# RWKV-5 attention and SwiGLU on one Trainium2 core: unpadded k and r tiles, and another order of the first steps

## The chip, the cores and the metric

The kernel runs on one core of one Trainium2 chip. The metric is the device time of one execution in microseconds (us). The kernel before took 755.13 us, the median of three runs (754.04 to 755.39).

## The reference

The first half is a linear attention with a decay for each channel, over 4 batches, 8 heads, 768 positions and head dimension 48. The second half is a SwiGLU block over the 3072 rows of 384 that come out of it, with a hidden width of 1536.

```
state = zeros(B, H, D, D)
for t in range(S):                      # B, H, S, D = 4, 8, 768, 48
    cur = einsum('bhd,bhe->bhde', u * k[t], v[t])
    y[t] = einsum('bhd,bhde->bhe', r[t], state + cur)
    state = w * state + einsum('bhd,bhe->bhde', k[t], v[t])
x = y.transpose(0, 2, 1, 3).reshape(B * S, H * D)        # 3072 x 384
g = x @ w_gate                                           # 384 x 1536
out = (g * sigmoid(g) * (x @ w_val)) @ w_out             # 1536 x 384
```

The three weight matrices come as 64-bit floats, and the kernel makes 32-bit floats of them by work on their bits ("rounding").

## The kernel before, in words

The 768 positions are cut into 6 chunks of 128; with 4 batches that makes N = 24 tiles, tile i being chunk i // 4 of batch i % 4. For each tile the kernel does this, with all 8 heads side by side, two heads to a pair:

- `load` (L95) and `load_v` (L101) issue the DMAs of k, r and v on SP's queue. k and r come in rows of 48 numbers, 8 heads to a position; in the tile each head has 64 columns, 48 of data and 16 of zeros, so a pair fills 128 partitions once turned.
- `prepare` (L223), on POOL (GpSimd): khat = k * kscale and rhat = r * rscale (powers of the decay and their inverses, tables made at the start), rk = r * k and rk * u; then DVE (VectorE) sums rk to du, one number for each head and position.
- `turn` (L244): PE (TensorE) transposes khat and rhat, ACT (ScalarE) copies them to kT and rT. kT holds each head of a pair in its own half of the partitions, with zeros in the other.
- `diagonal` (L237): POOL fills At with du on its diagonal (identity times du, 128 x 1024).
- `scores` (L259), in two halves: PE multiplies kT and rT, DVE writes the results over At where the mask allows.
- `outputs` (L272): PE makes the tile's output from At and v, and from rT and the state Z; ACT copies it to xT.
- `update` (L299): PE makes khat times v, DVE adds it to Z, POOL scales Z by wL.

Two tiles make a group g of 256 rows for the second half. `gate_value` (L324) is one piece: 128 columns of the hidden width, 6 matmuls with wg and wv into one of two PSUM buffers (gv), a sigmoid on ACT, two products on DVE (L339, L340) into hT. `project` (L344) is a third of the output of one tile. A group has 12 gate/value pieces and 6 projection parts.

The weights are loaded in 18 chunks of 768 KB with three buffers (w_bits). `round_weights` (L137) takes one chunk through two instructions on ACT (w_mag, w_low: L151, L152), two on DVE (L155, L156) and an add on POOL (L157), all issued in one call, and then loads another chunk. The chunks come in the order of use: gate and value in turns for 256 columns, then the output matrix.

The order is written by hand, in the last loop of `fast`, over steps s (L375). Each engine runs its instructions in the order of the program. Step s does the diagonal of tile s - 1, prepares tile s + 1, turns tile s, scores tile s - 1, makes the outputs and the update of tile s - 2; in odd steps from 3 on it queues a new group. Between these parts there are five gaps, in which `feed` takes pieces from the front of one list, at most 3 a step in steps 3 to 7, 5 in steps 8 and 9, then 12. Two gaps round one chunk each, and `gate_value` rounds ahead of itself what it needs.

Of the kernel before, what the change touches and what calls it, by code (L numbers as in the profile page):

```python
# [15 lines left out]
P = 128  # L16
# [6 lines left out]
def fast(  # L23
# [26 lines left out]
    DP = 64  # L50
# [16 lines left out]
    wcol = cst.tile([P, HP], FP32, name="wcol")  # L67
    ub = cst.tile([P, H, D], FP32, name="ub")
    kscale = cst.tile([P, H, DP], FP32, name="kscale")
    rscale = cst.tile([P, H, DP], FP32, name="rscale")  # L70
    wL = cst.tile([P, HP, 2 * D], FP32, name="wL")
    sq = cst.tile([P, 8, HP], FP32, name="sq")
    bad = cst.tile([P, HP], FP32, name="bad")
    held = cst.tile([P, HP], FP32, name="held")
    badc = cst.tile([P, 1], FP32, name="badc")
    ones = cst.tile([P, 1], FP32, name="ones")
# [7 lines left out]
    Z = [cst.tile([P, HP, 2 * D], FP32, name=f"Z{b}") for b in range(B)]  # L84
    r_ld = [cst.tile([P, H, DP], FP32, name=f"r_ld{i}") for i in range(2)]
    k_ld = [cst.tile([P, H, DP], FP32, name=f"k_ld{i}") for i in range(2)]

    v_ld = [cst.tile([P, HP, VW], FP32, name=f"v_ld{i}") for i in range(4)]
    khat = [cst.tile([P, H, DP], FP32, name=f"khat{i}") for i in range(4)]
    rhat = [cst.tile([P, H, DP], FP32, name=f"rhat{i}") for i in range(2)]  # L90
    At = [cst.tile([P, H, P], FP32, name=f"At{i}") for i in range(2)]

    kT = [cst.tile([P, HP, 2, P], FP32, name=f"kT{i}") for i in range(2)]

    def load(i):  # L95
        c, b = divmod(i, B)
        rows = slice(P * c, P * (c + 1))
        for src, dst in ((k, k_ld[i % 2]), (r, r_ld[i % 2])):
            sp.dma_start(out=dst[:, :, 0:D], in_=src[b, :, rows, :].rearrange("h t d -> t h d"))
# [22 lines left out]
    AHEAD = 3  # L122
    bits = {}
    state = {"loaded": 0, "rounded": 0}

    def load_weights():
        n = state["loaded"]
        if n == len(chunks):
            return
        state["loaded"] += 1  # L130
        src = chunks[n][0].bitcast(INT32)
        bits[n] = three.tile([P, WN, 2], INT32, name="w_bits", tag="w_bits")
        sp.dma_start(
            out=bits[n][:].rearrange("p (c f) two -> p c (f two)", c=src.shape[1]), in_=src
        )

    def round_weights(count):  # L137

        for _ in range(count):
            n = state["rounded"]
            if n == len(chunks):
                return
            state["rounded"] += 1
            x = bits.pop(n)
            lo, hi = x[:, :, 0], x[:, :, 1]
            dst = chunks[n][1].bitcast(INT32)
            mag = two.tile([P, WN], INT32, name="w_mag", tag="w_mag")
            low = two.tile([P, WN], INT32, name="w_low", tag="w_low")  # L150
            act.activation(mag[:].bitcast(FP32), hi.bitcast(FP32), AF.Abs, scale=float(2.0**-112))  # L151
            act.activation(low[:], lo.bitcast(UINT32), AF.Copy, scale=float(2.0**-29))  # L152
            c = dst.shape[1]
            mag, low, hi = (t.rearrange("p (c f) -> p c f", c=c) for t in (mag[:], low[:], hi))
            dve.tensor_scalar(dst, hi, -(1 << 31), None, ALU.bitwise_and)  # L155
            dve.scalar_tensor_tensor(dst, mag, 3, dst, ALU.logical_shift_left, ALU.bitwise_or)  # L156
            pool.tensor_tensor(dst, dst, low, ALU.add)  # L157
            load_weights()


    pool.memset(wcol[:], 1.0)
    for t in k_ld + r_ld:
        dve.memset(t[:, :, D:DP], 0.0)
    for t in v_ld:
        dve.memset(t[:, :, D:64], 0.0)
    for e in range(2):
        sp.dma_start(out=wcol[64 * e : 64 * e + D, :], in_=w.rearrange("(a e) d -> e d a", e=2)[e])
# [6 lines left out]
    for n in range(AHEAD):  # L174
        load_weights()

    make_identity(nc, ident[:])
    dve.tensor_scalar(held[:], wcol[:], W_LOW, W_HIGH, ALU.max, ALU.min)
# [3 lines left out]
    pw = two.tile([P, HP, P + 1], FP32, name="pw", tag="hT")  # L182
    ipw = two.tile([P, HP, P], FP32, name="ipw", tag="hT")
    dve.memset(pw[:, :, P : P + 1], 1.0)
    dve.tensor_copy(pw[:, :, P - 1 : P], held[:].unsqueeze(2))
    for l in range(7):
        n = 1 << l
        f = sq[:, l, :].unsqueeze(2).to_broadcast([P, HP, n])
        dve.tensor_mul(pw[:, :, P - 2 * n : P - n], pw[:, :, P - n : P], f)
    dve.reciprocal(ipw[:], pw[:, :, 0:P])  # L190
    for src, dst in ((pw[:, :, 1 : P + 1], kscale), (ipw[:], rscale)):
        t_ps = ps_a.tile([P, HP, P], FP32, name="t_ps", tag="a")
        for a in range(HP):
            pe.transpose(t_ps[:, a, :], src[:, a, :], ident[:])
        act.copy(dst[:].rearrange("p h d -> p (h d)"), t_ps[:].rearrange("p a x -> p (a x)"))  # L195
    pool.memset(wL[:], 0.0)
    for e in range(2):
        q = slice(64 * e, 64 * e + 64)
        dve.tensor_copy(
            wL[q, :, D * e : D * (e + 1)], sq[q, 7, :].unsqueeze(2).to_broadcast([64, HP, D])  # L200
        )
# [6 lines left out]
    for t in kT:  # L208
        for e in range(2):
            pool.memset(t[64 * e : 64 * e + 64, :, 1 - e, :], 0.0)  # L210
# [10 lines left out]
    dus, turned = {}, {}  # L221

    def prepare(i):  # L223
        kl, rl = k_ld[i % 2], r_ld[i % 2]
        rk = two.tile([P, H, D], FP32, name="rk", tag="rk")
        pool.tensor_mul(khat[i % 4][:], kl[:], kscale[:])  # L226
        pool.tensor_mul(rhat[i % 2][:], rl[:], rscale[:])  # L227
        pool.tensor_mul(rk[:], rl[:, :, 0:D], kl[:, :, 0:D])  # L228
        pool.tensor_mul(rk[:], rk[:], ub[:])  # L229
        du = three.tile([P, H], FP32, name="du", tag="du")  # L230
        dve.tensor_reduce(du[:], rk[:], axis=AX.X, op=ALU.add)  # L231
        dus[i] = du
        load_v(i)
        if i + 2 < N:
            load(i + 2)

    def diagonal(i):  # L237

        pool.tensor_mul(  # L239
            At[i % 2][:], ident[:].unsqueeze(1).to_broadcast([P, H, P]),  # L240
            dus.pop(i)[:].unsqueeze(2).to_broadcast([P, H, P]),
        )

    def turn(i):  # L244
        for nm, t in (("kT", khat[i % 4]), ("rT", rhat[i % 2])):
            tp = ps_a.tile([P, HP, P], FP32, name="tp", tag="a")
            for a in range(HP):
                pe.transpose(  # L248
                    tp[:, a, :], t[:, 2 * a : 2 * a + 2, :].rearrange("p e d -> p (e d)"), ident[:]
                )  # L250
            if nm == "kT":
                for e in range(2):
                    q = slice(64 * e, 64 * e + 64)
                    act.copy(kT[i % 2][q, :, e, :], tp[q])  # L254
            else:
                turned[i] = three.tile([P, HP, P], FP32, name=nm, tag=nm)
                act.copy(turned[i][:], tp[:])
# [41 lines left out]
    def update(i):  # L299
# [4 lines left out]
        ps = ps_a.tile([P, HP, 2 * D], FP32, name="u_ps", tag="a")  # L304
        for a in range(HP):
            pe.matmul(  # L306
                ps[:, a, :].rearrange("p (e d) -> p e d", e=2),
                kh[:, 2 * a : 2 * a + 2, :].rearrange("p e d -> p (e d)"),
                bass.AP(
                    tensor=vl.tensor, offset=vl[:, a, 0:1].offset,  # L310
                    ap=[list(vl[:].ap[0]), [64, 2], [1, D]],
                ),
                start=True, stop=True, skip_group_check=True,
            )
        if c == 0:
            dve.tensor_mul(z[:], ps[:], wL[:])
        else:
            dve.tensor_add(z[:], ps[:], z[:])  # L318
            pool.tensor_mul(z[:], z[:], wL[:])  # L319


    hT = {}

    def gate_value(g, f):  # L324
        if g == 0:
            round_weights(2 * (f // 2) + 4 - state["rounded"])
# [17 lines left out]
    def project(g, j, part):  # L344
        c, b = divmod(2 * g + j, B)
        round_weights(len(chunks) - state["rounded"])
# [15 lines left out]
    todo = deque()  # L362

    def feed(n):
        for _ in range(min(n, len(todo))):
            todo.popleft()()

    def queue(g):
        for f in range(FC):
            todo.append(lambda g=g, f=f: gate_value(g, f))  # L370
            if g > 0 and f >= 2 and f < 8:
                todo.append(lambda g=g, n=f - 2: project(g - 1, n // 3, n % 3))

    prepare(0)
    for s in range(N + 2):  # L375

        per = [0] * 5 if s < 3 else [1, 0, 1, 0, 1] if s < 8 else [1] * 5 if s < 10 else [3, 2, 2, 3, 2]
        if 1 <= s <= N:
            diagonal(s - 1)
        if s + 1 < N:  # L380
            prepare(s + 1)
        if s < N:
            turn(s)
        round_weights(1 if s else 0)
        feed(per[0])
        if 1 <= s <= N:
            scores(s - 1, 0)
            feed(per[1])
            scores(s - 1, 1)
            feed(per[2])  # L390
        if s >= 2:
# [3 lines left out]
            feed(per[3])  # L395
            update(s - 2)
        round_weights(1 if s > 1 else 0)
        feed(per[4])
    feed(len(todo))
    for j in range(2):  # L400
        for part in range(3):
            project(N // 2 - 1, j, part)
# [413 lines left out]
```

## Time and profile before

| what | value |
|---|---|
| median of the runs | 755.13 us |
| the profiled execution | 753.81 us |
| its span, from the first to the last instruction | 752.1 us |
| PE busy in the span | 704.4 us |
| POOL, DVE, ACT busy | 203.6, 218.1, 153.9 us |
| mean granted TensorE clock | 0.981 |

Times in rows of the trace are microseconds from the span's start, or ns where "mean" is said. A row of groups reads: line, engine, operation, output from inputs, shapes, count, then busy time and mean ns of one, then the idle time of that engine just before them and what ended it. A row of waits reads: who waited for whom, us in total, times, longest. PEld is the loading of the stationary operand, which overlaps PE. One fp32 matmul leaves two records, so a gate/value piece of six matmuls shows as x12. An engine that is idle off the path to the end costs nothing.

### The profile page before, as it was taken

Reading aid. Unit: us, or ns where it says so; the run is one execution under the profiler, and the core shown is the slowest. Engines: PE = TensorE matmul, PEld = TensorE weight load, DVE = VectorE, ACT = ScalarE, POOL = GpSimd, SP = SyncE. Lnnn points to the kernel's source line nnn. Section 1 sums busy time; section 2 is a strip of 40 time slices with the busy share of each in tenths; the row PEclk is TensorE's granted clock in tenths of the full one; section 3 lists DMA queues with packets and bytes.
Section 4 is the critical chain, followed back from the end, with each engine's and each line's share of the span. In section 5 each row is a group of like instructions: output and inputs, shape, how many; then the busy total and the mean of one; then the engine's idle time right before and its main releaser. Section 6 shows DMA issues by size and latency. Waiting matters only on the chain.

```text
span 752.1 us, 10222 instructions
## 1 busy us (share of the span) xinstructions
PE 704.4 (94%) x4298; PEld 563.0 (75%) x4298; DVE 218.1 (29%) x448; ACT 153.9 (20%) x305; POOL 203.6 (27%) x168
## 2 busy tenths in 40 slices
PE   2775978999999999999999999999999999999997
PEld 1654867878878778778778778778778778777773
DVE  4255654523222222223123213123213212212120
ACT  2541634311112111102111112111112112111110
POOL 5865667650303030303030303030302311000000
PEclk9988989999999999999999999999999999999999
DMA  8565555121102020102020201020100000000000
GB/s 213 112 152 147 165 161 156 32 43 33 32 11 43 1 43 11 31 11 43 1 53 1 44 11 31 12 42 5 38 22 1 23 12 2 12 10 2 10 11 24
DMA packets 85767, 33.98 MB, mean 45 GB/s; under 512 B 76368, under 2 KB 79568, under 8 KB 85712
## 3 DMA queue, kind: packets, MB, share of 16 engines
q1 hardware_dynamic: 82256, 28.52, 16.2%
q10 hardware_dynamic: 3456, 4.72, 1.8%
q8 instruction: 36, 0.59, 0.3%
q14 instruction: 19, 0.16, 0.1%
HBM read 28.51 MB, written 4.72 MB: 44 GB/s over the span
## 4 chain that ended last, share of the span: by engine, by line
PE 85%; POOL 6%; DVE 5%; issue 2%; ACT 1%; DMA 0%; SPq 0%; DVEq 0%; POOLq 0%
PE gv L332 48%; PE o_ps L351 25%; PE y_ps L293 4%; PE s_ps L263 4%; PE tp L248 2%; PE u_ps L306 2%; POOL At L239 2%; POOL rhat L227 1%; POOL khat L226 1%; POOL rk L229 1%; POOL rk L228 1%; DVE wv L156 1%; DVE wg L156 1%; DVE wv L155 1%; DVE wg L155 1%
## 5 line engine op out<-in xcount | busy, mean ns | idle before, releaser
L332 PE MATMUL gv<-xT,wg 128*128 128x256 f32 x864 | 217.5, 389 | 19.1 <-DVE hT L340 16.8
L332 PE MATMUL gv<-xT,wv 128*128 128x256 f32 x864 | 212.7, 383 | 0.0
L332 PEld LDWEIGHTS gv<-xT,wg 128*128 128x128 f32 x864 | 161.5, 193 | 50.4 <-issue 20.0
L351 PE MATMUL o_ps<-wo,hT 128*128 128x384 f32 x576 | 197.4, 487 | 0.6 <-ACT o_sb L357 0.6
L332 PEld LDWEIGHTS gv<-xT,wv 128*128 128x128 f32 x864 | 166.7, 193 | 23.5
L339 DVE TENSOR_TENSOR sg<-sg,gv 128x256 f32<-128x256 f32 x144 | 60.5, 420 | 359.3 <-ACT sg L338 359.3
L351 PEld LDWEIGHTS o_ps<-wo,hT 128*128 128x128 f32 x576 | 107.7, 190 | 62.0 <-ACT o_sb L357 1.2
L338 ACT ACTIVATE sg<-gv 128x256 f32<-128x256 f32 x144 | 55.3, 384 | 427.2 <-PE gv L332 427.2
L319 POOL TENSOR_TENSOR Z<-Z,wL 128x384 f32<-128x384 f32 x16 | 16.5, 1032 | 342.2 <-DVE Z L318 342.2
L340 DVE TENSOR_TENSOR hT<-sg,gv 128x256 f32<-128x256 f32 x144 | 60.5, 420 | 4.9
L239 POOL TENSOR_TENSOR At<-ident,du 128x1024 f32<-128x1024 f32 x24 | 45.5, 1898 | 37.6 <-PE y_ps L293 37.6
L263 PEld LDWEIGHTS s_ps<-rT,kT 128*128 128x128 f32 x384 | 50.4, 197 | 7.0 <-DVE At L267 0.7
L263 PE MATMUL s_ps<-rT,kT 128*128 128x128 f32 x384 | 51.0, 281 | 0.3 <-DVE At L267 0.3
L267 DVE COPY_PREDICATED At<-mask,s_ps 128x512 f32<-128x512 int32 x48 | 34.0, 732 | 41.5 <-PE s_ps L263 41.5
L231 DVE TENSOR_REDUCE du<-rk 128x8 f32<-128x384 f32 x24 | 13.3, 553 | 100.0 <-POOL rk L229 100.0
L293 PE MATMUL y_ps<-At,v_ld 128*32 128x128 f32 x768 | 36.7, 283 | 5.2 <-issue 2.8
L293 PEld LDWEIGHTS y_ps<-At,v_ld 128*32 128x32 f32 x768 | 30.4, 113 | 6.5 <-issue 3.6
L226 POOL TENSOR_TENSOR khat<-k_ld,kscale 128x512 f32<-128x512 f32 x24 | 30.5, 1271 | 5.4 <-ACT kscale L195 5.4
L227 POOL TENSOR_TENSOR rhat<-r_ld,rscale 128x512 f32<-128x512 f32 x24 | 30.6, 1274 | 2.0 <-ACT outside L218 2.0
L254 ACT COPY kT<-tp 64x512 f32<-64x512 f32 x48 | 27.9, 580 | 12.6 <-PE tp L248 11.3
L293 PE MATMUL y_ps<-rT,Z 128*32 128x128 f32 x480 | 30.1, 279 | 0.0
L293 PEld LDWEIGHTS y_ps<-rT,Z 128*32 128x32 f32 x480 | 19.3, 109 | 8.3 <-issue 7.8
(60 smaller groups left out, 318.4 us busy)
## 6 DMA issues: line engine op xcount, KB each, us to landing
k_ld<-in_k_dram SPq DMA_DIRECT2D x24, 192.0 KB, 3.1
r_ld<-in_r_dram SPq DMA_DIRECT2D x24, 192.0 KB, 3.5
w_bits<-in_moe_w_gate_dram SPq DMA_DIRECT2D x6, 768.0 KB, 4.6
w_bits<-in_moe_w_val_dram SPq DMA_DIRECT2D x6, 768.0 KB, 4.6
v_ld<-in_v_dram SPq DMA_DIRECT2D x48, 96.0 KB, 2.7
w_bits<-in_moe_w_out_dram SPq DMA_DIRECT2D x6, 768.0 KB, 4.3
out_dram<-o_sb ACTq DMA_DIRECT2D x24, 192.0 KB, 1.9
ub<-in_u_dram SPq DMA_DIRECT2D x1, 192.0 KB, 4.5
```

Of the source, the lines that this page charges most:

```text
L226: pool.tensor_mul(khat[i % 4][:], kl[:], kscale[:])
L227: pool.tensor_mul(rhat[i % 2][:], rl[:], rscale[:])
L239: pool.tensor_mul(At[i % 2][:], ident[:].unsqueeze(1).to_broadcast([P, H, P]), dus.pop(i)[:].unsqueeze(2).to_broadcast([P, H, P]),)
L254: act.copy(kT[i % 2][q, :, e, :], tp[q])
L263: pe.matmul(ps[:, n, :], kT[i % 2][:, a, e, :], turned[i][:, a, :], start=True, stop=True, skip_group_check=True,)
L267: dve.copy_predicated(At[i % 2][:, 4 * half : 4 * half + 4], mask[:].bitcast(INT32).unsqueeze(1).to_broadcast([P, HP, P]), ps[:],)
L293: pe.matmul(ps[32 * q : 32 * q + 32, cc, :], *rows[q][n], start=(n == 0), stop=(n == len(rows[q]) - 1), skip_group_check=True,)
L332: pe.matmul(gv[:, o, :].rearrange("p (i t) -> p i t", i=2), wt[:, c, P * f : P * (f + 1)], xT[:, 2 * g % NX : 2 * g % NX + 2, c, :], start ...
L338: act.activation(sg[:], gv[:, 0, :], AF.Sigmoid)
L339: dve.tensor_mul(sg[:], sg[:], gv[:, 0, :])
L340: dve.tensor_mul(hT[g][:, f, :], sg[:], gv[:, 1, :])
L351: pe.matmul(ps[:], hT[g][:, f, P * j : P * (j + 1)], wo[:, f, :], start=(f == 0), stop=(f == FC - 1),)
```

## The change

Everything is in `fast`; the general path behind it is not touched.

**Unpadded tiles.** k, r, khat, rhat, kscale and rscale have 48 columns for each head, so a turned pair fills 96 partitions; wcol, wL, Z, kT and rT have 96 partitions. The products on POOL run over 384 columns, not 512. [...] Memsets of the padding and of kT go.

**Tables.** Both tables are turned from the same powers pw, and the reciprocal is taken by DVE behind the transpose, from PSUM, over 384 columns. Before, DVE took it ahead of the transpose over 512.

**u products.** `prepare` is split: `own_product` (rk, rk * u, du) and `scale` (khat, rhat, loads). For tiles 0 and 1 the u products stand ahead of the first khat; afterwards ahead of khat of the same tile.

**Diagonal.** For tiles 0 to 5 the diagonal is made by eight activations on ACT, one a head, from then on by POOL as before.

**Rounding.** It is cut into three parts with a counter each; one call does POOL's part of a chunk that has its DVE part, DVE's part of the next one, and ACT's part of one further on. The load of another chunk is issued with DVE's part.

**Order of pieces.** The list is searched for the first piece whose weights have been issued (`need`), so pieces of group 1 run between those of group 0. Groups 0 and 1 have no projection parts between their pieces; those of group 0 follow all at once, ahead of group 2. A table says for each gap of steps 0 to 8 whether to round (R) or to feed (F): five pieces a step from step 4.

```diff
-    DP = 64
+    D2 = 2 * D
...
+    def round_act():
+        n = next_chunk("act")
+        if n is not None:
...
+            act.activation(
+                mags[n][:].bitcast(FP32), hi.bitcast(FP32), AF.Abs, scale=float(2.0**-112)
+            )
+            act.activation(lows[n][:], lo.bitcast(UINT32), AF.Copy, scale=float(2.0**-29))
...
+    def round_weights():
+
+        if done["dve"] > done["pool"]:
+            round_pool()
+        if done["act"] > done["dve"]:
+            round_dve()
+        round_act()
...
+    own_product(0)
+    own_product(1)
...
     def diagonal(i):
 
-        pool.tensor_mul(
-            At[i % 2][:], ident[:].unsqueeze(1).to_broadcast([P, H, P]),
-            dus.pop(i)[:].unsqueeze(2).to_broadcast([P, H, P]),
-        )
+        du = dus.pop(i)
+        if i < 6:
+            for h in range(H):
+                act.activation(At[i % 2][:, h, :], ident[:], AF.Identity, scale=du[:, h : h + 1])
+        else:
...
                 for e in range(2):
-                    q = slice(64 * e, 64 * e + 64)
-                    act.copy(kT[i % 2][q, :, e, :], tp[q])
+                    act.activation(
+                        kT[i % 2][:, :, e, :], tp[0:D2], AF.Identity, scale=own[:, e : e + 1]
+                    )
...
     def feed(n):
-        for _ in range(min(n, len(todo))):
-            todo.popleft()()
+        for _ in range(n):
+            ready = [k for k, (need, _) in enumerate(todo) if need <= done["pool"]]
+            if ready:
+                todo.pop(ready[0])[1]()
...
+    EARLY = [
+        ("R", "", "", "", "R"),
...
+        ("R", "", "RF", "F", "F"),
+        ("RF", "F", "RF", "F", "F"),
...
-        per = [0] * 5 if s < 3 else [1, 0, 1, 0, 1] if s < 8 else [1] * 5 if s < 10 else [3, 2, 2, 3, 2]
```

What stands on PE from the outputs of tile 1 (step 3) to the outputs of tile 2 (step 4), before: tp are the transposes, s_ps the scores, y_ps the outputs, u_ps the update, and a pair of gv rows (wg, wv) is one piece.

```order
L293 MATMUL y_ps<-At_114,v_ld_104 32x128 x16
L306 MATMUL u_ps<-v_ld_104,khat_108 128x96 x4
L332 MATMUL gv<-xT,wg 128x256 x3
L332 MATMUL gv<-xT,wv 128x256 x3
L248 MATMUL tp<-ident,khat_107 128x128 x4
L248 MATMUL tp<-ident,rhat_111 128x128 x4
L332 MATMUL gv<-xT,wg 128x256 x3
L332 MATMUL gv<-xT,wv 128x256 x3
L263 MATMUL s_ps<-rT,kT_116 128x128 x8
L332 MATMUL gv<-xT,wg 128x256 x3
L332 MATMUL gv<-xT,wv 128x256 x3
L293 MATMUL y_ps<-At_113,v_ld_105 32x128 x16
```

And in the changed kernel, from the step's transposes on:

```order
L285 MATMUL tp<-ident,khat_108 96x128 x4
L285 MATMUL tp<-ident,rhat_112 96x128 x4
L366 MATMUL gv<-xT,wg 128x256 x3
L366 MATMUL gv<-xT,wv 128x256 x3
L299 MATMUL s_ps<-rT,kT_117 128x128 x4
L366 MATMUL gv<-xT,wg 128x256 x3
L366 MATMUL gv<-xT,wv 128x256 x3
L299 MATMUL s_ps<-rT,kT_117 128x128 x4
L366 MATMUL gv<-xT,wg 128x256 x3
L366 MATMUL gv<-xT,wv 128x256 x3
L329 MATMUL y_ps<-At_114,v_ld_106 32x128 x16
```

Between the transposes and the outputs of step 4 there are three pieces where there were two, one of them between the score halves, and two follow behind the outputs.

What stands on ACT in step 3, before (w_mag and w_low are a chunk's rounding, sg the sigmoid):

```order
L254 COPY kT_116<-tp 64x4x128 x2
L257 COPY rT<-tp 128x512
L151 ACTIVATE w_mag<-w_bits 128x768
L152 ACTIVATE w_low<-w_bits 128x768
L297 COPY xT<-y_ps 128x384
L151 ACTIVATE w_mag<-w_bits 128x768
L152 ACTIVATE w_low<-w_bits 128x768
L338 ACT_TABLE_LOAD
L338 ACTIVATE sg<-gv 128x256
```

And now:

```order
L271 ACTIVATE At_114<-ident,du 128x128 x8
L288 ACTIVATE kT_117<-tp,own 96x4x128 x2
L293 COPY rT<-tp 96x512
L151 ACTIVATE w_mag<-w_bits 128x768
L154 ACTIVATE w_low<-w_bits 128x768
L151 ACTIVATE w_mag<-w_bits 128x768
L154 ACTIVATE w_low<-w_bits 128x768
L333 COPY xT<-y_ps 128x384
L372 ACT_TABLE_LOAD
L372 ACTIVATE sg<-gv 128x256 x2
```

Eight instructions of the diagonal have come ahead, both chunks stand ahead of the copy to xT, and two sigmoids follow it instead of one.

What stands on POOL behind the start, before (rk_... rows are the u products):

```order
L226 TENSOR_TENSOR khat_107<-k_ld_101,kscale 128x512
L227 TENSOR_TENSOR rhat_111<-r_ld_99,rscale 128x512
L228 TENSOR_TENSOR rk<-r_ld_99,k_ld_101 128x384
L229 TENSOR_TENSOR rk<-rk,ub 128x384
L226 TENSOR_TENSOR khat_108<-k_ld_102,kscale 128x512
L227 TENSOR_TENSOR rhat_112<-r_ld_100,rscale 128x512
L228 TENSOR_TENSOR rk<-r_ld_100,k_ld_102 128x384
L229 TENSOR_TENSOR rk<-rk,ub 128x384
L239 TENSOR_TENSOR At_113<-ident,du 128x1024
```

And now:

```order
L187 TENSOR_TENSOR rk<-r_ld_100,k_ld_102 128x384
L188 TENSOR_TENSOR rk<-rk,ub 128x384
L187 TENSOR_TENSOR rk<-r_ld_101,k_ld_103 128x384
L188 TENSOR_TENSOR rk<-rk,ub 128x384
L260 TENSOR_TENSOR khat_108<-k_ld_102,kscale 128x384
L261 TENSOR_TENSOR rhat_112<-r_ld_100,rscale 128x384
L260 TENSOR_TENSOR khat_109<-k_ld_103,kscale 128x384
L261 TENSOR_TENSOR rhat_113<-r_ld_101,rscale 128x384
L172 TENSOR_TENSOR wg<-wg,w_low 128x3x256
```

The u products of tiles 0 and 1 have come ahead of the first khat, and where the diagonal stood there is now the add of the first chunk.

More of the change, by code (lines that the diff above doesn't have):

```diff
@@ L121, in fast @@
     WN = 6 * P
-    AHEAD = 3
-    bits = {}
-    state = {"loaded": 0, "rounded": 0}
-    def load_weights():
[L127 to L134, printed above, removed]
-        )
[L137 to L147, printed above, removed]
+    NW = len(chunks)
@@ L148, in round_weights, with round_dve @@
+    def round_dve():
+        n = next_chunk("dve")
+        if n is not None:
             dst = chunks[n][1].bitcast(INT32)
[L149 to L152, printed above, removed]
             c = dst.shape[1]
-            mag, low, hi = (t.rearrange("p (c f) -> p c f", c=c) for t in (mag[:], low[:], hi))
+            hi = bits.pop(n)[:, :, 1].rearrange("p (c f) -> p c f", c=c)
+            mag = mags.pop(n)[:].rearrange("p (c f) -> p c f", c=c)
@@ L218, in fast, with scale @@
     act.copy(outside, n_ps[0:1, 0, 0:1])
[L221 to L232, printed above, removed]
+    turned = {}
+    def scale(i):
+        pool.tensor_mul(khat[i % 4][:], k_ld[i % 2][:], kscale[:])
+        pool.tensor_mul(rhat[i % 2][:], r_ld[i % 2][:], rscale[:])
         load_v(i)
@@ L394, in fast @@
                 queue((s - 3) // 2)
[L395 removed]
+            gap(s, 3)
             update(s - 2)
[L397 to L398 removed]
+        gap(s, 4)
+    assert done["pool"] == NW
     feed(len(todo))
[L400 to L402 removed]
+    for p in range(6):
+        project(N // 2 - 1, p // 3, p % 3)
 @with_exitstack
```

174 lines of the change are left out of this document (112 added, 62 removed).

## The prediction

> **What bounds the kernel now.** I read the stretches first, cut where TensorE stops waiting (at 123.6 us); columns: busy us of PE, PEld, DVE, ACT, POOL with instruction counts, then granted clock, DMA share and GB/s.
>
> ```profile
> 0.00:123.60 123.60, 83.77 (x618) 69.98 (x619) 58.89 (x109) 50.21 (x77) 82.06 (x72) 0.90 0.60 155
> 123.60:752.10 628.50, 620.67 (x3680) 493.02 (x3680) 159.16 (x340) 103.68 (x228) 121.50 (x97) 1.00 0.10 24
> 20.00:40.00 20.00, 13.85 (x104) 11.82 (x103) 6.04 (x9) 9.34 (x14) 15.21 (x12) 0.91 0.57 118
> ```
>
> Behind 123.6 us PE is busy 620.67 of 628.50 us at clock 1.00: only less work there, or work done sooner, shortens that part. Ahead of it PE is idle for 40 us and runs at clock 0.90, and no engine is full (POOL 82 of 124). So a loop of waits sets the pace. The chain, one step of it:
>
> ```profile
> 46.07 1.90 POOL At L239
> 47.97 1.22 POOL khat L226
> 49.19 1.22 POOL rhat L227
> 50.41 0.97 POOL rk L228
> 51.45 1.00 POOL rk L229
> 52.48 0.55 DVE du L231
> 53.03 0.87 DVE wv L155
> 54.00 0.96 DVE wv L156
> 54.95 1.29 DVE At L267 x2
> 56.24 0.44 DVE Z L316
> 58.78 1.72 issue
> 60.50 1.90 POOL At L239
> ```
>
> POOL does the diagonal and the four products, DVE waits for the last of them (du), then does both rounding chunks of the step in its queue, and POOL's adds of these chunks (under "issue") come before the next diagonal. The step takes 60.50 - 46.07 = 14.4 us and each lap crosses POOL, DVE and POOL again. The waits of the same stretch say it too (us in total, times, longest):
>
> ```profile
> DVE du L231 <- POOL rk L229: 58.3, 9, 8.3
> ```
>
> Then the chain where PE takes over, whose pieces are also my prices of PE work (a gate/value piece is x12, two tiles of transposes x8, both score halves x16, one update x8), and one output tile without the state term from the timeline:
>
> ```profile
> 105.18 4.89 PE gv L332 x12
> 110.07 0.87 PE tp L248 x8
> 110.95 2.59 PE gv L332 x12
> 113.54 1.78 PE s_ps L263 x16
> 117.92 1.73 PE y_ps L293 x55
> 123.62 4.21 PE gv L332 x12
> 142.73 0.86 PE u_ps L306 x8
> 62.29 1.10 PE L293 MATMUL y_ps<-At,v_ld 128*32 128x128 f32 x32
> ```
>
> A piece costs 2.59 us, but 4.89 or 4.21 right after a wait. From the order, by 123.62 us PE has done steps 0 to 6, and of step 7 its transposes, scores, outputs and update (scores 0 to 6, outputs 0 to 5, updates 0 to 5), and 12 pieces.
>
> **The change part by part.** *The loop.* Staging puts a chunk's three parts in three successive calls, so POOL's adds are of a chunk that DVE finished earlier. In steps 1 to 6 the diagonal (1.90) leaves POOL for ACT; khat and rhat fall from 512 to 384 columns, the width of rk, so from 1.22 to about 0.96.
>
> ```profile
> L157 POOL TENSOR_TENSOR wv<-wv,w_low 128x768 int32<-128x768 int32 x6 | 10.9, 1822 | 13.7 <-DVE wv L156 13.7
> L151 ACT ACTIVATE w_mag<-w_bits 128x768 f32<-128x768 f32 x18 | 16.5, 916 | 13.6 <-DVE wv L156 6.5 <-DVE wg L156 5.2 <-DVE wo L156 1.8
> L152 ACT ACTIVATE w_low<-w_bits 128x768 int32<-128x768 uint32 x18 | 16.4, 911 | 6.1 <-POOL wv L157 2.6 <-POOL wg L157 2.5 <-POOL wo L157 1.0
> L254 ACT COPY kT<-tp 64x512 f32<-64x512 f32 x48 | 27.9, 580 | 12.6 <-PE tp L248 11.3
> L297 ACT COPY xT<-y_ps 128x384 f32<-128x384 f32 x24 | 11.5, 479 | 57.8 <-PE y_ps L293 57.8
> L338 ACT ACTIVATE sg<-gv 128x256 f32<-128x256 f32 x144 | 55.3, 384 | 427.2 <-PE gv L332 427.2
> L340 DVE TENSOR_TENSOR hT<-sg,gv 128x256 f32<-128x256 f32 x144 | 60.5, 420 | 4.9
> ```
>
> POOL's step with two chunks: 0.96 x 2 + 0.97 + 1.00 + 1.82 x 2 = 7.5 us. ACT's: two chunks 2 x (0.92 + 0.91) = 3.65, kT and rT three times 0.58 = 1.75 (I take 1.9, because two of them now carry a scale by partition), and eight new 128x128 instructions for the diagonal. No row shows one. 384 columns take 0.479 and 256 take 0.384, so 128 would be 0.28 by that slope (8 x 0.28 = 2.2 us); the upper end is the 256-column price, 8 x 0.384 = 3.1. I take 2.7, the middle, because the slope knows no per-partition scale. ACT's step is 3.65 + 1.9 + 2.7 = 8.25 us and ACT, not POOL, becomes the fullest engine of steps 1 to 3. The Trainium skill ("ScalarE: Activation LUTs", section "What ACT_TABLE_LOAD costs") charges 186 ns plus 0.833 ns a column, 93 ns more for each pointer operand, and lets neighbours overlap by 93 ns; that is about 2.3 us for the eight, and the sum would come out about 1.2 us lower. No run here shows such an instruction yet.
>
> *The start.* The first rounding on ACT now stands behind the cast of the flag, and the flag's matmul behind DVE's reciprocal and two du, which wait for POOL's four early products. All of ACT is queued behind this cast.
>
> ```profile
> 7.94 1.09 PE L194 MATMUL t_ps<-ident,pw 128*128 128x128 f32 x4 [7.94 <-DVE pw L189]
> L190 DVE RECIPROCAL ipw<-pw 128x512 f32<-128x512 f32 x1 | 3.4, 3354 | 0.0
> 11.57 0.16 DVE L213 TENSOR_TENSOR bad<-held,wcol 128x4 f32<-128x4 f32 x1
> 12.88 0.14 ACT L218 CAST outside<-n_ps 1x1 int32<-1x1 f32 x1
> ```
>
> Both table transposes now follow each other, to about 7.94 + 2 x 1.09 = 10.1; the reciprocal of 384 columns is 3.35 x 384/512 = 2.5, to 12.6; wL at Z's price 0.5, two du 1.1, to 14.2; from "bad" to the end of the cast it took 13.02 - 11.57 = 1.45 with a wait in it, I take 1.0: ACT is free at 15.2 us.
>
> *The first piece.* From there ACT does chunk 0 (1.8), kT and rT (1.9), chunks 1 and 2 (3.65), to 22.5; three steps of 8.25, to 47.3; two copies of outputs (0.96), to 48.2. The second of these copies ends the wait of the first gate/value piece. What ACT still waits for comes on top: in the rows above it waited 13.6 + 6.1 = 19.7 us on 18 chunks, 1.1 each, or 9.9 us on the nine chunks here. Staging removes most of that; I keep 1.8. So the first piece starts at 50 us, bounds 46.7 (no waits, diagonal at 2.2) and 58 (all waits). Before, it started at 44.8:
>
> ```profile
> 44.82 1.49 PE L332 MATMUL gv<-xT,wg 128*128 128x256 f32 x6
> ```
>
> The early steps thus gain nothing by themselves; three times two chunks are rounded earlier in exchange.
>
> *Steps 4 to 8.* Five pieces a step from two groups, instead of three: PE 5 x 2.59 + 0.87 + 1.78 + 1.73 + 0.86 = 18.2 us a step. ACT with three chunks: 5.5 + 1.9 + 2.7 + 0.48 + 5 x 0.384 = 12.5; POOL 9.4; both below 18.2, so PE sets the pace and the waits of the loop hide under it. The tightest place is the step's first sigmoid: ahead of it on ACT stand the diagonal 2.7, kT and rT 1.9 and a chunk 1.83, then come the sigmoid 0.38 and DVE's two products 0.84, 7.7 us in all from the step's start; the third piece wants the same buffer at 0.87 + 2 x (2.59 + 0.89) = 7.8. That is no margin, so I take 2 us of waits over these steps.
>
> *Catching up.* At 50 us PE has done four transposes, three scores, two outputs and one update. It has left, to the state of 123.62 us: 12 x 2.59 + 4 transposes 3.5 + 4 scores 7.1 + outputs 2 x 1.10 + 2 x 1.73 = 5.7 + 5 updates 4.3 = 51.6 us. The first piece follows a wait and pays 4.89 - 2.59 = 2.3 once; in exchange the piece at 123.62 (4.21) runs at 2.59, 1.6 less.
>
> *The rest.* Unpadding leaves PE's moving columns as they are (128 in transposes and scores, 96 in updates), so PE's work stays. DMA runs stay 48 numbers at the source: I cost it at nothing. On SP's queue the loads of chunks 3 and 4 now stand ahead of v of tile 2 and k, r of tile 4, not behind; v of tile 2 is read two steps later, k of tile 4 by POOL in step 3, some 15 us on, so the queue hides it. The kT copies grow from 64 to 96 partitions, same columns; ACT is busy 103.68 of 628.50 there and hides it. Pieces done early empty the list sooner: a new group then starts right behind its outputs, which cost this:
>
> ```profile
> PE gv L332 <- ACT xT L297: 2.4, 4, 0.6
> ```
>
> The list (39 items done at the end of step 9, not 23; 24 offered and 18 added in two steps) first runs dry in step 15, not 19: two more waits of 0.6, 1.2 us.
>
> *Sum.* 50.0 + 51.6 + 2.3 + 2.0 + (628.5 - 1.6) + 1.2 = 734.0 us of span against 752.1, so 18.1 less. The profiled run took 753.8 with its 1.7 around the span: 735.7. The median shown, 755.1, lies 1.3 higher: 737.
>
> **The rivals.** *Late and ragged:* ACT keeps its old waits, the first piece starts at 58, and the sigmoids in steps 4 to 8 cost PE up to 4 us more than I took: 745 to 749. For it: w_low needs the buffer that POOL's add two chunks earlier frees, so ACT still waits on POOL. Against: POOL has only 7.5 us of work in a step of 8.25.
>
> *Light ACT:* diagonal at its lower bound, no waits: first piece at 46.7, no raggedness, 737 - 3.3 - 2.0 = 731.7, some us less if the piece starts warm.
>
> *DMA sets the pace (slower):* what 123.6 us of loads brought, 155 GB/s x 123.6 us = 19.2 MB, must now come by about 106 us, 181 GB/s; and by 50 us the first nine chunks, six k, six r, four v and u:
>
> ```profile
> w_bits<-in_moe_w_gate_dram SPq DMA_DIRECT2D x6, 768.0 KB, 4.6
> k_ld<-in_k_dram SPq DMA_DIRECT2D x24, 192.0 KB, 3.1
> ```
>
> (9 x 768 + 17 x 192 KB, about 10.4 MB, 215 GB/s.) If the queue can't bring more than the 155 GB/s of before, the gain is gone: 19.2 MB end at 124 us again, 755; at 145 GB/s they end at 132 us, 763. That is the point from which it decides. Against: DMA was busy only 0.60 of the time at 155, which makes 258 GB/s at full share; the worst stretch, 118 GB/s at 0.57, still makes 207, and 10.4 MB at 207 GB/s take 50 us, just where ACT ends anyway.
>
> **How the numbers follow.** A difference of 0.2% (1.5 us) is about what a measurement of this kernel tells from no change. Chances: forecast (731 to 742) 0.62, light ACT below that 0.08, late and ragged 0.20, DMA at its old rate within 0.2% 0.04, slower 0.06. So faster 0.90, same 0.04, slower 0.06. The range 729 to 749 covers the bounds of the first piece and the ragged case, and leaves out the DMA cases and a lucky start.
>
> **What would show it.** Right: first gv near 50 us; POOL's At absent before the seventh; PE 0.95 busy or more from then on at clock 1.00; step pitch about 8 us in steps 1 to 3 and 18 in steps 4 to 7; PE still busy for some 620 us behind its state of 123.62; six waits for xT. Wrong: gv waiting for hT by several us a step; ACT waiting for DMA of w_bits; or eight diagonals well over 3.1 us.

## The result and the profile after

| what | before | after |
|---|---|---|
| median of 4 runs each | 755.26 us | 736.34 us |
| lowest and highest | 754.04 to 755.65 | 735.78 to 738.54 |
| the profiled execution, its span | 753.81, 752.1 us | 738.54, 736.8 us |
| mean granted TensorE clock | 0.981 | 0.981 |

The ratio of the times is 0.9758 (95% interval 0.9735 to 0.978): 18.9 us faster. The forecast was 737.0, in a range of 729 to 749. The profiled execution of after is the highest of its four, 2.2 us above the median; all rows of after below are of this execution.

The stretches of after, cut at 20 and 40 us, then at the first gate/value piece (47.60) and at the piece (123.92) that stands nearest to the cut of before at 123.6. Columns as in the prediction.

```profile
20.00:40.00 20.00, 13.08 (x94) 11.94 (x93) 14.21 (x16) 18.13 (x40) 19.76 (x14) 0.66 0.99 256
47.60:123.92 76.32, 70.64 (x476) 61.75 (x477) 43.25 (x69) 37.57 (x77) 38.16 (x28) 0.95 0.44 116
123.92:736.80 612.88, 603.93 (x3660) 477.20 (x3660) 146.13 (x320) 96.34 (x216) 106.31 (x93) 1.00 0.09 22
```

Where before needed 628.5 us from 123.6 to its end, after needs 612.88 from 123.92, 15.6 less. By then it has done 19 gate/value pieces where before had 12, but not yet the outputs and the update of step 7: 7 x 2.59 - 1.73 - 0.86 = 15.5 us of PE's work done sooner. Ahead of 123.92 PE is idle for 31.7 us where before it was for 40, and 26 of them lie ahead of the first piece; from there to 123.92 PE is busy 70.64 of 76.32 us, or 0.93. But look at POOL between 20 and 40 us: 19.76 of 20, where before it had 15.21. ACT, which the forecast took for the fullest engine, has 18.13.

One lap of the early steps on the chain of work that ended last (start, duration, engine, what):

```profile
28.35 1.67 POOL rk L187
...
30.10 1.01 POOL rk L188
31.10 0.95 POOL khat L260
32.05 0.95 POOL rhat L261
33.01 0.87 POOL wv L172
...
33.97 1.49 issue
35.46 1.82 POOL wg L172
37.29 1.68 POOL rk L187
```

The lap is 37.29 - 28.35 = 8.94 us, and every row of it is POOL's or POOL's "issue". The chain no longer crosses to DVE and ACT. The waits of PE, in total, times, longest:

```profile
PE gv L366 <- ACT xT L333: 9.9, 8, 5.8
PE gv L366 <- DVE hT L374: 5.1, 2, 4.2
```

The long wait for xT ends at the first piece, the long wait for hT at 123.92. Behind 130 us the trace has six waits for xT, 0.6 us each.

Two pieces follow a long wait and are slow, and the update has become shorter (chain rows):

```profile
47.60 5.49 PE gv L366 x12
71.03 0.68 PE u_ps L342 x8
123.92 5.27 PE gv L366 x12
```

### The profile page after: what moved, and what is told of

The parts are those of the page before. It is cut to its first block, busy times and chain, and to the rows that moved or that the text cites. A ratio compares the mean times of both kernels' runs of the same rounds, so it can differ in the third digit from the quotient of the medians.

```text
span 736.8 us, 10255 instructions
## 1 busy us (share of the span) xinstructions
PE 696.1 (94%) x4298; PEld 558.2 (76%) x4298; DVE 223.4 (30%) x443; ACT 165.1 (22%) x352; POOL 184.0 (25%) x159
## 4 chain that ended last, share of the span: by engine, by line
PE 88%; POOL 5%; issue 2%; DMA 1%; DVE 1%; ACT 1%; SPq 0%; POOLq 0%
PE gv L366 49%; PE o_ps L384 25%; PE y_ps L329 5%; PE s_ps L299 5%; PE tp L285 2%; PE u_ps L342 2%; DMA r_ld<-in_r_dram 1%; POOL rk L187 1%; POOL wo L172 1%; POOL wg L172 1%; POOL rhat L261 1%; POOL rk L188 1%; POOL khat L260 1%; ACT xT L333 1%; DVE wo L164 0%
## 5 line engine op out<-in xcount | busy, mean ns | idle before, releaser
L355 POOL TENSOR_TENSOR Z<-Z,wL 96x384 f32<-96x384 f32 x16 | 16.1, 1008 | 359.4 <-DVE Z L354 359.4
L299 PEld LDWEIGHTS s_ps<-rT,kT 96*128 96x128 f32 x384 | 52.5, 204 | 6.3 <-ACT rT L293 0.3
L299 PE MATMUL s_ps<-rT,kT 96*128 96x128 f32 x384 | 52.8, 287 | 0.0
L273 POOL TENSOR_TENSOR At<-ident,du 128x1024 f32<-128x1024 f32 x18 | 34.1, 1894 | 38.0 <-PE y_ps L329 38.0
L288 ACT ACTIVATE kT<-tp,own 96x512 f32<-96x512 f32 x48 | 30.1, 675 | 1.3 <-PE tp L285 0.5
L329 PE MATMUL y_ps<-rT,Z 96*32 96x128 f32 x480 | 30.2, 278 | 0.0
L187 POOL TENSOR_TENSOR rk<-r_ld,k_ld 128x384 f32<-128x384 f32 x24 | 27.6, 1148 | 4.3 <-DMA r_ld<-in_r_dram 4.3
L390 ACT COPY o_sb<-o_ps 128x384 f32<-128x384 f32 x24 | 11.5, 479 | 73.7 <-PE o_ps L384 73.7
L260 POOL TENSOR_TENSOR khat<-k_ld,kscale 128x384 f32<-128x384 f32 x24 | 24.0, 999 | 13.3 <-PE u_ps L342 13.3
L333 ACT COPY xT<-y_ps 128x384 f32<-128x384 f32 x24 | 11.5, 478 | 63.7 <-PE y_ps L329 63.7
```

Of the source, the lines that this page charges most:

```text
L187: pool.tensor_mul(rk[:], rl[:], kl[:])
L260: pool.tensor_mul(khat[i % 4][:], k_ld[i % 2][:], kscale[:])
L273: pool.tensor_mul(At[i % 2][:], ident[:].unsqueeze(1).to_broadcast([P, H, P]), du[:].unsqueeze(2).to_broadcast([P, H, P]),)
L288: act.activation(kT[i % 2][:, :, e, :], tp[0:D2], AF.Identity, scale=own[:, e : e + 1])
L299: pe.matmul(ps[:, n, :], kT[i % 2][:, a, e, :], turned[i][:, a, :], start=True, stop=True, skip_group_check=True,)
L329: pe.matmul(ps[32 * q : 32 * q + 32, cc, :], *rows[q][n], start=(n == 0), stop=(n == len(rows[q]) - 1), skip_group_check=True,)
```

## The experiments

Each is an edit of the kernel after, unless it says otherwise. The times are medians, the ratios are to the kernel before, run beside them on the same chip.

| run | time us | ratio, 95% interval |
|---|---|---|
| after | 736.34 | 0.9758 [0.9735, 0.978] |
| e1_narrow_only | 745.17 | 0.9884 [0.9864, 0.9904] |
| e2_three_pieces | 734.71 | 0.9737 [0.9721, 0.9753] |
| e3_unstaged | 734.41 | 0.9733 [0.9717, 0.9749] |
| e4_diagonal_on_pool | 741.59 | 0.9828 [0.9812, 0.9845] |
| e5_act_diagonal_to_8 | 735.70 | 0.9746 [0.973, 0.9763] |
| e6_without_kr_loads | 736.34, one execution | |
| e8_unstaged_diagonal_to_8 | 731.14 | 0.9688 [0.9672, 0.9704] |
| e9_narrow_and_act_diagonal | 735.24 | 0.974 [0.9724, 0.9757] |
| e10_old_order_diagonal_to_8 | 732.85 | 0.9704 [0.9687, 0.972] |
| e11_four_w_low | 730.72 | 0.9681 [0.9664, 0.9697] |
| e12_unstaged_to_8_three_w_low | 731.01 | 0.9684 [0.9668, 0.9701] |

### Narrow tiles alone (e1)

The kernel before with the unpadded tiles and the new tables, and nothing of the new order: whole chunks rounded in one call, the diagonal on POOL, pieces from the front of the list at the old rate.

```diff
-        if done["dve"] > done["pool"]:
-            round_pool()
-        if done["act"] > done["dve"]:
-            round_dve()
         round_act()
+        round_dve()
+        round_pool()
...
-        if i < 6:
+        if i < 0:
```

> Only the 48-column tiles, 96 partitions and the new tables; rounding, pieces, u products and diagonal in the order of before. Theory A (the gain is PE work done early, which the order makes possible): POOL's lap of 14.4 us loses 2 x 0.27 = 0.54 us in some seven laps, so about 751 us (748 to 754). Theory B (narrower tiles are the gain): about 738 us.

Measured: 745.17 us, about 9 of the 18.9 us. The diagonals on the chain, of before and then of e1:

```profile
31.62 1.89 POOL At L239
```

```profile
28.62 1.90 POOL At L270
42.51 1.90 POOL At L270
```

The loop of waits starts 3.0 us earlier, the start being shorter. A lap takes 42.51 - 28.62 = 13.9 us, 0.5 less than before. And each update is shorter by the same 0.18 us as in after (below). So the narrow tiles alone, with their tables, bring half of the gain.

### The pace of steps 1 to 3 (e4 and e6)

e4 gives all diagonals back to POOL; e6 leaves out the loads of k and r for tiles 2 to 5 only.

```diff
-        if i < 6:
+        if i < 0:
```

> The changed kernel with every diagonal on POOL. If POOL sets the pace of steps 1 to 3 (its trace shows it busy 19.8 of 20 us there), each gets 1.9 us longer, the first piece starts at about 53 us and the time is 742 us (739 to 745). If ACT sets it (as the prediction had it), ACT's step falls by 2.4 us, the first piece starts near 46 us or earlier and the time is 735 us or less. If DMA sets it (busy 0.99 of the time there), nothing moves: 736 us.

```diff
         for src, dst in ((k, k_ld[i % 2]), (r, r_ld[i % 2])):
+            if 2 <= i < 6:
+                continue
```

> The changed kernel without the loads of k and r of tiles 2 to 5 (these tiles use what the buffers hold), 1.6 MB less of the 8.8 MB that DMA moves from 14 to 48 us. If DMA sets the pace of steps 1 to 3, the first piece comes some 5 us earlier, near 42.5. If POOL does, the step stays 8.95 us and the first piece starts at 46.5 to 47.6.

Measured: 741.59 us for e4, 5.3 slower than after, and 736.34 for e6, no change. The stretch of e4 and its chain, then the stretch of e6 and two rows of its chain:

```profile
20.00:40.00 20.00, 8.50 (x71) 7.54 (x71) 13.82 (x15) 10.21 (x15) 19.84 (x14) 0.71 0.97 252
```

```profile
27.80 1.83 POOL wg L172
29.63 2.57 POOL At L273
...
38.57 1.83 POOL wg L172
...
52.55 4.49 PE gv L366 x12
```

```profile
20.00:40.00 20.00, 13.30 (x127) 11.95 (x128) 15.22 (x17) 18.37 (x40) 19.81 (x14) 0.74 0.78 226
```

```profile
25.99 1.83 POOL wg L174
34.94 1.83 POOL wg L174
```

In e4 POOL is full (19.84) while ACT falls to 10.21, the lap grows to 38.57 - 27.80 = 10.8 us and the first piece slips from 47.60 to 52.55. Take work from ACT and nothing gets faster; give it to POOL and each lap pays about all of it. So POOL sets the pace of these steps. In e6 the DMA share falls from 0.99 to 0.78 and the lap stays at 8.95: the DMA share of 0.99 did not bound the lap.

### Staging (e3), and why a POOL instruction is not always as long as its row

```diff
-        if done["dve"] > done["pool"]:
-            round_pool()
-        if done["act"] > done["dve"]:
-            round_dve()
         round_act()
+        round_dve()
+        round_pool()
```

> The changed kernel, but each call rounds one chunk through ACT, DVE and POOL at once. Theory A: POOL again waits for DVE's part of the same chunk, up to 2 x 1.9 us in a step of 9, the first piece comes at about 53 us, not 47.6, and behind it the 18 us of PE cover the waits: 742 us (738 to 748). Theory D (staging carries the gain by itself): 750 us or more.

Measured: 734.41 us, not slower than after. POOL by the timeline (start, duration, line, what; in brackets its idle time and what ended it), first one row of after, then three of e3:

```profile
32.96 2.54 POOL L172 TENSOR_TENSOR wv<-wv,w_low 128x768 int32<-128x768 int32 x1
```

```profile
33.06 1.83 POOL L172 TENSOR_TENSOR wv<-wv,w_low 128x768 int32<-128x768 int32 x1 [0.96 <-DVE wv L164]
36.22 1.83 POOL L172 TENSOR_TENSOR wg<-wg,w_low 128x768 int32<-128x768 int32 x1 [1.33 <-DVE wg L164]
38.01 1.01 POOL L185 TENSOR_TENSOR rk<-r_ld,k_ld 128x384 f32<-128x384 f32 x1
```

Staged, POOL hardly waits, but one add takes 2.54 instead of 1.83, and the first rk 1.67 (the chain of after, above) instead of 1.01. That is 1.4 us a lap, the difference between the 7.5 us of work that I had summed and the lap of 8.94. In after DVE is at work at just these moments:

```profile
32.65 1.17 DVE L164 SCALAR_TENSOR_TENSOR wg<-w_mag,wg 128x768 int32<-128x768 int32 x1
...
36.02 2.08 DVE L164 SCALAR_TENSOR_TENSOR wv<-w_mag,wv 128x768 int32<-128x768 int32 x1
```

This instruction took 0.96 in the rows of before. Here it overlaps POOL's add of 35.46 and ends only at 38.10, 0.8 behind the add's end. Unstaged, DVE is done before POOL's add starts, so both keep their short times, and POOL waits for DVE (the brackets): the lap of e3 is 9.9 us (36.22 - 26.35, the row of the add one lap earlier, below) with no add and no rk lengthened, against 8.94 with both lengthened. Staging traded a wait for a collision.

```profile
26.35 1.80 POOL wg L172
```

The first piece comes 3.0 us later in e3 (at 50.56), but it takes 2.86 us, not 5.49. That gives 2.6 of the 3.0 back. The rest comes near 120 us, where e3 has a wait of 2.6 us for hT and a piece of 4.51, and after a wait of 4.2 and a piece of 5.27. The granted clock (last figures but two) of these pieces, of after and then of e3:

```profile
47.60:53.09 5.49, 5.49 (x14) 4.36 (x15) 0.00 (x0) 1.25 (x1) 1.31 (x2) 0.50 0.51 172
...
123.92:129.19 5.27, 5.27 (x16) 3.91 (x20) 3.25 (x6) 0.00 (x0) 0.00 (x0) 0.53 0.00 0
```

```profile
50.56:53.42 2.86, 2.85 (x14) 2.52 (x15) 2.35 (x4) 1.25 (x1) 1.70 (x3) 1.00 0.42 84
```

The two slow pieces ran at a granted clock of 0.50 and 0.53; PE had waited 5.8 and 4.2 us ahead of them. The one of e3 followed a wait of 0.61 us and ran at 1.00. So the 4.2 us wait at 123.92 cost another 5.27 - 2.59 = 2.7 behind it in this execution; in those of e4 and e6 the piece behind the same 4.2 us wait took 4.51, so 1.9.

### Five pieces or three (e2)

The table of steps 3 to 9 gets three pieces a step, the rate of before, rounding at the same places.

```diff
-        ("R", "", "RF", "F", "F"),
-        ("RF", "F", "RF", "F", "F"),
+        ("R", "", "R", "", "F"),
+        ("RF", "", "RF", "", "F"),
+        ("RF", "", "RF", "", "RF"),
+        ("RF", "", "RF", "", "RF"),
+        ("RF", "", "RF", "", "RF"),
         ("RF", "F", "RF", "F", "RF"),
-        ("RF", "F", "RF", "F", "RF"),
-        ("RF", "F", "RF", "F", "RF"),
-        ("RF", "F", "RF", "F", "RF"),
+        ("F", "F", "F", "F", "F"),
```

> The changed kernel, but in steps 3 to 9 the pieces are taken at the rate of before (1, then 3, from step 8 on 5 a step); staged rounding, diagonal on ACT and u products stay. Theory A (PE is the limit from its first piece on, whichever piece it is): a step of 3 x 2.59 + 5.2 = 13.0 us still just covers ACT (12.6) and POOL, so only some waits come back, 740 us (737 to 745). Theory C (five pieces a step from two groups carry the gain): about 750 us.

Measured: 734.71 us, ratio 0.9737 where after has 0.9758, and the intervals overlap. Five pieces a step are not what brought the gain: pieces that aren't fed early are fed later, at no loss here.

### The diagonal on ACT alone, in the old order (e9, e10)

e9 is e1 with one number changed, e10 has it at 8.

```diff
-        if i < 0:
+        if i < 6:
```

> The narrow tiles in the order of before (745.2 us), with the diagonals of tiles 0 to 5 on ACT. Theory F (what counts is POOL's work in the loop, not the new order): the lap of 13.9 loses 1.9 us, six laps, 11 us less: 735 us (732 to 738), as good as the whole change. Theory A (the order of rounding and pieces is needed to keep PE fed): 742 us or more, since DVE's wait for du and POOL's for DVE stay.

Measured: 735.24 us, the whole of the change's gain without its order. Products and first piece on its chain:

```profile
20.46 0.97 POOL rk L185
...
28.88 0.97 POOL rk L185
...
41.08 2.63 PE gv L366 x12
```

The one lap that the chain shows falls from 13.9 us in e1 to 8.4, since the diagonal now runs on ACT while POOL goes on with its products, and the first piece starts at 41.08, before that of after. e9 pays later, with hT waits of 11.3 us in all. So theory F had the time right but not the way to it: the lap lost 5.5 us, not 1.9, and a part of that is lost again. Once the diagonal is on ACT, staging, the mixing of two groups and the early u products together are worth nothing that these runs can tell from zero. With the diagonal on POOL they are worth 3.6 us: e4 is the new order and e1 the old one, 741.59 against 745.17, and their intervals are apart. The diagonal's move in turn brings 9.9 us in the old order (e1 to e9) and 5.3 in the new (e4 to after). The parts of the change overlap and do not add up.

> Narrow tiles in the order of before, diagonals of tiles 0 to 7 on ACT; it differs from e8 (731.1 us) only in the order: u products, rounding calls a step, five pieces from two groups. Theory F (only POOL's work in the loop counts): 731 us (730 to 733), as e8. Theory A in what is left of it (the order feeds PE more evenly): 734 us or more, with several us of waits for hT left that e8 doesn't have (0.9).

Measured: 732.85 us, ratio 0.9704. Beside e8 below (0.9688) the intervals overlap: what is left of the new order is 1.2 us by the ratios, and from these intervals anything between nothing and about 3 us.

### What held the sigmoid back at 116 to 124 us (e5, e11)

The 4.2 us wait of after ends at 123.92. The chain to it, then the same place on POOL (the scaling of Z, ahead of the chain's first row here), DVE and ACT by the timeline:

```profile
110.58 1.77 POOL wo L172
112.35 1.85 POOL At L273
114.20 1.68 POOL rk L187
...
119.19 2.48 POOL wo L172
...
122.50 0.38 ACT sg L372
```

```profile
109.34 1.24 POOL L355 TENSOR_TENSOR Z<-Z,wL 96x384 f32<-96x384 f32 x1 [10.79 <-DVE Z L354]
```

```profile
109.76 5.26 DVE L164 SCALAR_TENSOR_TENSOR wo<-w_mag,wo 128x768 int32<-128x768 int32 x1
```

```profile
121.69 0.90 ACT L154 ACTIVATE w_low<-w_bits 128x768 int32<-128x768 uint32 x1 [5.68 <-POOL wo L172]
```

Two suspects. One: DVE's instruction is held for 5.26 us while POOL runs three of its own back to back, and the products for hT stand behind it. Two: ACT's w_low waits 5.68 us for a buffer that POOL's add has yet to read; that add stands behind the diagonal and the products, all of these behind the scaling of Z, for which POOL idles 10.79 us; and the sigmoid stands behind w_low. e5 takes the diagonals of tiles 6 and 7 off POOL, which shortens the first and a part of the second; e11 gives w_low four buffers, which removes the second alone.

```diff
-        if i < 6:
+        if i < 8:
```

> The changed kernel with the diagonals of tiles 6 and 7 on ACT too. In its trace POOL does Z, a rounding add and the diagonal without a pause from 109.3 to 114.2 us, DVE's rounding instruction lies across all of it (5.26 us, not 0.96), and PE then waits 5.1 us for hT and runs the next piece cold (2.7 more). Theory E (DVE's instruction can't go on while POOL is busy): without the diagonal there, most of these 7.8 us go, 730 us (728 to 733). Rival (ACT's queue is what delays the sigmoid): 2.4 us more on ACT in steps 7 and 8 keep the wait or lengthen it, 736 to 740 us.

```diff
+    four = ctx.enter_context(tc.tile_pool(name="four", bufs=4))
...
-            lows[n] = two.tile([P, WN], INT32, name="w_low", tag="w_low")
+            lows[n] = four.tile([P, WN], INT32, name="w_low", tag="w_low")
```

> The changed kernel with four buffers for w_low, not two, and nothing else. Theory G (near 115 to 122 us ACT stops at w_low until POOL has added the chunk two before, POOL's add stands behind Z, which waits for PE, and the sigmoid behind w_low is late): the 4.2 us wait for hT and its cold piece go, 5 to 7 us less, 730 us (728 to 732). Rival (DVE's long rounding instruction delays hT by itself): 735 to 737 us, the wait stays.

Measured: e5 735.70 us, e11 730.72. In e5 the DVE instruction gets shorter, but w_low, now behind a diagonal on ACT, still waits for POOL just ahead of the late sigmoid:

```profile
108.50 3.41 DVE L164 SCALAR_TENSOR_TENSOR wo<-w_mag,wo 128x768 int32<-128x768 int32 x1
```

```profile
118.58 0.89 ACT L154 ACTIVATE w_low<-w_bits 128x768 int32<-128x768 uint32 x1 [1.50 <-POOL wo L172]
```

5.26 - 3.41 = 1.85 is the length of the diagonal (1.89) that went. The collision is shown, but a wait of 3.5 us for hT remains, and a slow piece behind it. In e11 the long DVE instruction, the waits for hT, and the same piece:

```profile
107.08 5.26 DVE L165 SCALAR_TENSOR_TENSOR wo<-w_mag,wo 128x768 int32<-128x768 int32 x1
```

```profile
PE gv L367 <- DVE hT L375: 2.1, 2, 1.2
```

```profile
118.25 2.83 PE gv L367 x12
```

The DVE instruction still takes 5.26 us in e11, yet the long wait is gone and the piece is not slow (granted clock 1.00). So the buffers were the cause of the long wait. What the collision cost PE here is the short one, 0.8 us at 115.95 in after, which e11 has too. The buffers also held up the first piece: in after ACT's last w_low ahead of it stands behind POOL's add until 46.28, and in e11 it runs at 45.01, so that the first piece starts at 46.30, not 47.60 (of these 1.3 us, 0.3 were there in POOL's laps before). Together the short supply of w_low cost after 5.6 us by the medians.

### The best versions (e8, e12)

Unstaged rounding with the diagonal on ACT to tile 7 (e8), and the same with three w_low buffers (e12).

> Unstaged rounding and the diagonals of tiles 0 to 7 on ACT. The unstaged kernel took 734.4 us with 2.8 us of waits for hT and one cold piece (1.9) near 120 us. Theory E: these go, 730 us (728 to 732). Rival (that wait comes from rounding in one call, whatever POOL does): 734 us.

> e8 (unstaged, diagonals to tile 7 on ACT, 731.1 us) with three buffers for w_low. Little is left there to take away, 0.9 us of waits for hT. Theory G: 730 to 731 us. Rival (ACT running further ahead only moves its wait): 731 to 732 us.

Measured: 731.14 and 731.01 us. Unstaged, a third buffer adds nothing; staged, more buffers bring 5.6 us. e8, e11 and e12 are 5 us faster than after, and no interval tells them apart.

## Why the prediction was right, and where its steps were not

The time, 736.34 against 737.0, is closer than its terms deserve; the agreement is in part luck. Of the sum 50.0 + 51.6 + 2.3 + 2.0 + 626.9 + 1.2 = 734.0, these terms were measured otherwise:

- **The first piece** started at 47.60, not 50.0 (-2.4), inside its bounds of 46.7 and 58.
- **Its slowness** after the wait was 5.49 - 2.59 = 2.9, not 2.3 (+0.6). It differs between executions: in e4 and e6 the first piece took 4.49 and 4.53.
- **Waits in steps 4 to 8** were 0.6 for xT, 5.1 for hT and 2.7 for the slow piece at 123.92, 8.4 in all, not 2.0 (+6.4). This is the mis-sized term. I had allowed for a sigmoid that is late by its own queue; the runs showed the mechanism that I had named only under "late and ragged", w_low waiting for the buffer of POOL's add. That rival had its wait right and its place in part: the wait stood ahead of the first piece too (e11), but made the start no later than forecast.
- **Updates** were missed. "PE's work stays" fails: an undisturbed update fell from 0.86 to 0.68 us. The rows below are of all updates of after and of before, and the second figure is the mean ns of one. The moving columns are 96 in both, but the stationary operand has 96 columns and not 128: its loading falls from 203 to 175 ns and the matmul from 287 to 258. That the one makes the other is read from these rows; no run isolates it. By the chain's figures the 19 updates behind the first piece give 19 x 0.18 = 3.4 us (-3.4). Transposes, whose stationary operand is as narrow now, did not get shorter (0.87 us in both).

```profile
L342 PE MATMUL u_ps<-v_ld,khat 128*96 128x96 f32 x160 | 18.0, 258 | 3.4 <-DVE At L303 3.4
L342 PEld LDWEIGHTS u_ps<-v_ld,khat 128*96 128x96 f32 x160 | 17.8, 175 | 5.5 <-DVE At L303 3.7 <-issue 0.2
```

```profile
L306 PE MATMUL u_ps<-v_ld,khat 128*128 128x96 f32 x160 | 22.6, 287 | 0.0
L306 PEld LDWEIGHTS u_ps<-v_ld,khat 128*128 128x128 f32 x160 | 21.9, 203 | 2.5 <-issue 1.6
```

With these, 734.0 - 2.4 + 0.6 + 6.4 - 3.4 = 735.2 of span, against 736.8 measured; 1.6 stay unassigned. A wrong +6.4 was almost covered by -2.4 and -3.4; that is the luck. The forecast also added 1.3 us because before's profiled run lay below its median; after's lies 2.2 above it.

**The step that failed** reads "ACT's step is 3.65 + 1.9 + 2.7 = 8.25 us and ACT, not POOL, becomes the fullest engine of steps 1 to 3." ACT's half of it held: 18.13 busy in 20 us at a lap of 8.94 is 8.1 a step. POOL's 7.5 was a sum of times measured when DVE's instruction with two inputs did not run beside them, and staging makes it run beside them. The lap was 8.94, set by POOL; e4 shows it. Before's trace had the collision already, outside of the laps that I had read: this instruction, 0.96 elsewhere, overlaps POOL's add of 90.80 to 92.62 there and ends 0.8 behind it.

```profile
91.62 1.83 DVE wv L156
```

The first piece came 2.4 us earlier all the same: the chain to it ends with POOL's add until 46.25, one w_low (0.91) and one copy (0.37). So an ACT sum that had the wrong engine came out near the time that the right one gave.

**Prices of ACT.** The eight diagonal instructions were forecast at 2.7 us (2.2 to 3.1), and took 2.43 (the timeline's row). kT with its scale by partition (a column of `own`, 1 on one head's partitions and 0 on the other's) takes 675 ns where the copy took 580. The Trainium skill's price ("ScalarE: Activation LUTs", section "What ACT_TABLE_LOAD costs"), from which the prediction worked out an estimate of about 2.3, was nearer than mine. Eight such instructions have seven overlaps between them, and with these the same figures give an estimate of 2.43. The Trainium skill's 93 ns for a pointer operand agree with the 95 between 675 and 580:

```profile
21.51 2.43 ACT L271 ACTIVATE At<-ident,du 128x128 f32<-128x128 f32 x8
```

```profile
L288 ACT ACTIVATE kT<-tp,own 96x512 f32<-96x512 f32 x48 | 30.1, 675 | 1.3 <-PE tp L285 0.5
```

**The start.** ACT was forecast to be free at 15.2 us; the cast stands at 15.07 to 15.22. The two further waits for xT behind 130 us came as forecast, six of 0.6 where before had four.

**DMA.** The rival that DMA keeps its old rate falls: 256 GB/s came between 20 and 40 us, where 118 came before, and e6 shows that even this did not set the lap. The 10.4 MB that the prediction wanted by 50 us are 208 GB/s, not 215, which changes nothing in it.

**The signs.** POOL's At was absent before the seventh tile, and the pitch of the steps was 8.94 and then 17.9 us (updates at 53.09 and 71.03), about as forecast. PE from the first piece to 123.92 was busy 0.93 at clock 0.95, where 0.95 at 1.00 had been the sign; the waits for hT, a sign of being wrong, came once with 4.2 us, not in every step.

**The trade.** "The early steps thus gain nothing by themselves; three times two chunks are rounded earlier in exchange" describes after rightly, but as a reason for the gain it falls with e9, which gets the same time in the old order. The gain comes from the narrow tiles (e1, 9 us) and from the diagonal leaving POOL (e9 against e1, about 10 us). Two places where the new order gives back what it wins are shown: the collision of DVE and POOL (1.4 us a lap) and the w_low buffers (5.6 us, e11). With four of these buffers the new order is 4.5 us faster than e9; whether e9 would gain from more buffers too was not run.

## What to carry to other kernels

When a loop of waits is opened by letting two engines run side by side, add up each engine's work again under overlap: durations read from rows in which the other engine did not run beside it can be too short, as POOL's 7.5 us for 8.94 were. Look for the instruction in an in-order queue that waits for a buffer and has urgent work behind it; two more buffers there brought 5.6 us, the reordering 3.6 with the diagonal on POOL and nothing clear of noise with it on ACT. And undo each part of a compound change alone, and beside the others: here one changed number on top of narrower tiles gave all of its gain, and each part was worth less once another was there.

## What the hardware showed that I had not expected

DVE's two-input instruction on SBUF and POOL's instructions do not share time. In after DVE's L164 started at 109.76 while POOL ran, and ended at 115.02, 0.8 us behind the end of POOL's third instruction in a row (114.20); POOL's next one, rk, took 1.68 us in place of 1.00. In e5, with one POOL instruction fewer, it ended 0.8 us behind the second. The Trainium skill ("SBUF — State Buffer", section "SBUF: two separate sides") says that the two engines' shared ports are an exclusive lock for a whole instruction, which a DVE instruction with two SBUF inputs needs against a POOL instruction that reads SBUF. The rows agree, and add that several POOL instructions in a row can keep it: 5.26 us for an instruction of 0.96. What lets DVE in at last no run shows: here it was ahead of the first rk, and in the lap above also ahead of an add (the rows at 32.65 and 32.96).
